# Three chained sequence models on one core: the order of the attention part rewritten, with five PSUM banks and a later copy

## The chip, the cores and the metric

The kernel runs on one core of a Trainium2 chip. Measured is the device time of one execution in microseconds; lower is better. A profile is one execution of its own, recorded by the hardware profiler; its times are the rows shown below.

## What is computed

Three models follow one another on 4 sequences of 768 positions (768 x 384 per sequence).

```python
# 1. delta-rule attention, 8 heads of 48, state 48 x 48 per head
k_n = k / (norm(k) + 1e-6)
for t in range(768):
    y[t] = q[t] @ state
    state = state + beta[t] * outer(k_n[t], v[t] - k_n[t] @ state)
# 2. Fourier mixing and an MLP
u = x + real(fft(fft(x, over positions), over features))
x = u + relu(layernorm(u) @ w_ch1) @ w_ch2          # 384 -> 1536 -> 384
# 3. token mixing with a phase, and a channel MLP
theta = x @ w_theta
u = x + w_tok_r @ (x * cos(theta)) + w_tok_i @ (x * sin(theta))
out = u + relu(u @ w_ch)
```

All in float32. Large matmuls take each operand as a high and a low part and add three products (`mm3`, L84), so weights and inputs are split first.

## The kernel before

**Attention in chunks.** The recurrence is cut into chunks of 64 positions, 12 per sequence. For each chunk the inverse of a triangular 64 x 64 matrix is needed; it is made of two 32 x 32 blocks solved at once on VectorE and joined by small matmuls. The class `Front` has one method for each kind of step, and a number says which piece it works on:

- `k`, `q`, `g` (`gram`, L228): load transposed keys (L245), multiply them with themselves (`k`), with the queries (`q`) or both (`g`), and copy the products from PSUM into the tile `KQ` on ScalarE (L252, L255, L257, L259; L261 on GpSimd). Number d = 0 to 23 is a pair of chunks for all heads; four of them make a solve. `k` of d % 4 below 2 loads into the two buffers `kt`; the others borrow the buffers `u`, which the weight pieces use as well.
- `s` (`solve`, L263): w = 0 to 5. Transposes `KQ` (L272), then runs 30 steps of two dependent VectorE instructions (L309, L312) and a last product (L313). Tiles `T`, `TN`, `TT` have one buffer, `KQ` two.
- `j` (`solved`, L317): two transposes of the result into `TN` and `TT` (L321, L323).
- `l` (`load`, L362): four loads (L368, L370) and a mask on GpSimd (L372).
- `c` (`chunks`, L375): for pair d: loads v (L384), scales it on GpSimd (L385), first product `pa` (L390), its copy to `A` (L393), copies of `TT` into `YU` (L395, by `copy`, L356, on ScalarE for d in `COPY_ACT`, else on VectorE), second product `pt` with that copy as operand (L399), more copies (L401, L402), third product `pw` (L406) and its copy (L408).
- `n` (`scan`, L410): chunk g = 0 to 47, in order: product `pu` (L425), copies (L426, L427), new state `ps` (L436) and its copies (L437, L438), outputs `py` (L447), which every second scan copies (L452, L454) and stores (L455). Scan g uses pair g // 2, and pair d the solve d // 4.
- `f`: load the Fourier constants (L470). `w1` and `W1` (`convert`, L693): split one of 24 weight pieces (`Split.steps`, L106): load 384 KB (L120), first step on ScalarE (L123), VectorE (L124 to L130), three matmuls (L132 to L134), copies (L131, L135). `W1` may be issued on an engine only behind the last instruction of the latest solve there.

**The order.** `PLAN` (L66) lists all these steps; `attention_steps` (L701) runs the list, and "|" and every twelfth scan give control back. What is listed is a rank: the framework's scheduler goes through a simulated time and, on each engine and queue, takes the instruction of the lowest rank that it believes ready. The result is a fixed order for each engine, and on the chip each engine keeps to it. The list runs until scan 11 (the first sequence); then the Fourier inputs of the first sequence are made on VectorE (`fourier_inputs`, L472), and the MLP blocks begin: 12 blocks (256 positions each) of 12 steps, each step an `ffn_up` (L666) and an `ffn_down` (L678). After each step the list is run on to its next "|" (`attend`, L754), so the rest of the attention lies between matmuls of the MLP. Pieces of weights not yet converted are converted by the loop when needed: all 24 by step 5 of block 0. `LEAD` (L58) says at which steps of a block the next block's three preparations are ranked: loads, transform and norm, and transposes (`prepare_2`, L654: L661 to L663). When the attention is done, the weights of the third model are split in the same places; then the third model follows (`TokenMix.run`).

**PSUM.** Eight banks: two for the scan, one called `mw`, three in the ring `g`, and two accumulators `pc0` and `pc1` that `ffn_down` uses from the first block on. `mw()` (L219) gives a bank to each small product of the attention: until scan 11 every third goes to `mw` and the others to the ring `g`, behind it all to `mw`. The matmuls of the weight pieces use the ring too.

Of the kernel before, what the change touches and what calls it, by code (L numbers as in the profile page):

```python
# [10 lines left out]
F32 = mybir.dt.float32  # L11
# [31 lines left out]
NKT = 2  # L43
NYT = 8
BLOCKED = 0
COPY_ACT = (0, 1, 2, 3, 4, 5)
DIAG_ACT = (0, 1)
FOFF = 0
NZ = 9
# [4 lines left out]
AHEAD = {(0, 0): 1, (0, 1): 1, (0, 2): 1}  # L54
MIXACT = False
NMW = 1
MWT = 3
LEAD = (0, 4, 11)  # L58
LEAD_0 = (5, 7, 11)
LATE = {4: 1, 7: 1, 10: 1}  # L60
MIXAT = (11, 0)
# [1 line left out]
STRIDE = 2  # L63
ACTL = 2
NST = 2
PLAN = """k0 k3 k2 k1 q2 w1 g7 q0 l0 q1 q3 f l1 g4 s0 g5 g6 j0 c0 c1 n0 n1 n2 l2 W1 W1 W1 w1  # L66
 W1 n3 c2 l3 c3 W1 W1 W1 g9 W1 W1 w1 n4 g10 W1 n5 s1 j1 l4 g8 W1 W1 g11 c4 n6 n7 W1 n8
 W1 l5 n9 l6 c5 n10 W1 W1 n11 c6 s2 | l7 c7 j2 n12 n13 n14 n15 g13 g15 l8 c8 g12 g14 l9 c9 s3
 | | n16 n17 l10 | n18 n19 l11 c10 | c11 g19 | | g17 g18 n20 n21 g16 n22 j3 l12 c12 | n23 l13 |
 c13 n24 | | n25 l14 s4 n26 c14 n27 l15 c15 | g20 g21 g22 g23 n28 n29 l16 j4 c16 s5 | n30 n31 w1 |  # L70
 l17 c17 n32 n33 | l18 c18 n34 | n35 | l19 c19 n36 j5 | | n37 | l20 n38 n39 l21 c20 c21 | n40 n41
 l22 c22 n42 | n43 l23 c23 | n44 n45 | | n46 n47"""
SCAN_UP = (0, 0)
CHUNK_UP = (0, 0)
SOLVE_UP = (0, 0)
FDVE = 2
EVERY = 1
TCARGS = {"schedule_with_timeline_sim": True}
# [80 lines left out]
class Front:  # L159
# [10 lines left out]
    B1 = [slice(r, r + 32) for r in (64, 0)]  # L170
    B2 = [slice(r + 32, r + 64) for r in (64, 0)]
    ROWS = (slice(0, 128), slice(0, 112))

    def __init__(self, tc, io, ident, x2scr):
        self.tc, self.nc, self.io, self.ident, self.x2scr = tc, tc.nc, io, ident, x2scr
        self.stage1, self.staged, self.turn, self.early, self.T = -1, 0, 0, True, {}
        self.nT, self.KQ, self.ysc, self.py, self.y, self.z, self.G = {}, {}, {}, {}, {}, {}, {}

    def open_attention(self, ctx):
# [38 lines left out]

    def mw(self, shape, name):  # L219
        self.turn += 1  # L220
        if self.early and self.turn % MWT:
            return self.psg.tile(shape, F32, tag="g", name=name)
        return self.psw.tile(shape, F32, tag="mw", name=name)

    def mm(self, o, l, r):
        self.nc.tensor.matmul(o, l, r, start=True, stop=True, skip_group_check=True)  # L226
# [129 lines left out]
    def copy(self, d, o, i):  # L356
        if d in COPY_ACT:
            self.nc.scalar.activation(o, i, AF.Copy)
# [16 lines left out]
    def chunks(self, d):  # L375

        nc, mm, sol = self.nc, self.mm, self.sol
        FE, TK, B1, B2 = self.FE, self.TK, self.B1, self.B2
        TT, TN, nT, kq = self.W
        yu, x, y3 = self.YU[d % NYU], self.X[d % NX], self.Y3[d % NY3]  # L380
        i1 = 8 * (d % 4)
        n = slice(i1, i1 + 8)
# [8 lines left out]
        A = sol.tile([P, 8, 32], F32, tag="A", name=f"A{d}", bufs=2)  # L391
        for par in range(2):
            nc.scalar.activation(A[B2[par]], pa[B2[par]], AF.Copy)  # L393
        for par in range(2):
            self.copy(d, yu[B2[par], par, :, 32:64], TT[B2[par], n, :])  # L395
        pt = self.mw([P, 8, 32], f"pt{d}")
        for i in range(8):
            for par in range(2):
                mm(pt[B1[par], i, :], A[B2[par], i, :], yu[B2[par], par, i, 32:64])  # L399
        for par in range(2):  # L400
            self.copy(d, yu[B1[par], par, :, 0:32], TT[B1[par], n, :])  # L401
            nc.scalar.activation(yu[B1[par], par, :, 32:64], pt[B1[par]], AF.Copy, scale=-1.0)  # L402
        pw = self.mw([P, 8, C], f"pw{d}")
        for i in range(8):
# [336 lines left out]
def front(tc, top, io, ident, x2scr, mix):  # L741
# [6 lines left out]
    fr.init()  # L748
    steps = fr.attention_steps(PLAN)
    state = {"fed": 0}  # L750
# [62 lines left out]
    for n, (q, f) in enumerate(order):  # L813
        more = q + 1 < len(blocks)
        lead = LEAD if q else LEAD_0
        if f in lead and more:
# [299 lines left out]
```

## Time and profile before

| | |
|---|---|
| three timed runs | 961.49, 966.62, 970.60 us; median 966.62 |
| profiled execution, time | 964.93 us |
| its span, first to last instruction | 963.2 us |
| TensorE busy, share of the span | 884.4 us, 92% |
| VectorE, ScalarE, GpSimd busy | 66%, 44%, 32% |
| mean granted TensorE clock | 0.943 of full speed |

A busy TensorE isn't one at its peak, since matmuls overlap and their ends are modelled. The clock was granted at about one half from 24 to 72 us and at full speed from about 216 us.

### The profile page before, as it was taken

The numbers are of one execution on the slowest core, as the hardware profiler recorded it, in microseconds if no ns is written. First come the engines' busy times: TensorE is split into PE (matmuls) and PEld (weight loads), VectorE is DVE, ScalarE is ACT, GpSimd is POOL, SyncE is SP. The second block draws the span as 40 slices with busy tenths as digits, with TensorE's granted clock in tenths as the row PEclk, the third lists the DMA queues.
The fourth block names the chain that finished last, engine by engine and source line by source line (L and its number), as shares of the span: only waits on it lengthen the run. The fifth ranks groups of instructions, "written<-read, shape, count | busy, mean of one in ns | idle before, by whom it ended". The sixth has DMA issues, their size and how long they took to land.

```text
span 963.2 us, 23409 instructions
## 1 busy us (share of the span) xinstructions
PE 884.4 (92%) x9408; PEld 797.8 (83%) x9408; DVE 634.0 (66%) x1490; ACT 428.5 (44%) x1072; POOL 311.8 (32%) x422
## 2 busy tenths in 40 slices
PE   4659888789999999999999998999998999999998
PEld 4547566677988898988988997888997999999987
DVE  4989879946998872698231596878657866273411
ACT  4367676445534454345535322322556345162410
POOL 1201242323123014223313155554224545143321
PEclk7557897899999999999999999999999999999999
DMA  7324352323222014011313023233121311021000
GB/s 214 105 73 137 107 167 75 109 86 121 62 87 90 19 58 147 28 55 39 92 34 109 10 83 115 69 97 116 50 84 41 89 58 37 25 59 33 25 17 33
DMA packets 42204, 73.58 MB, mean 76 GB/s; under 512 B 6000, under 2 KB 26224, under 8 KB 42096
## 3 DMA queue, kind: packets, MB, share of 16 engines
q1 hardware_dynamic: 41328, 69.72, 24.2%
q0 software_dynamic: 768, 2.36, 0.9%
q8 instruction: 74, 1.21, 0.5%
q14 instruction: 34, 0.28, 0.1%
HBM read 57.91 MB, written 14.16 MB: 75 GB/s over the span
## 4 chain that ended last, share of the span: by engine, by line
PE 52%; DVE 24%; DMA 9%; ACT 6%; issue 4%; POOL 3%; SPq 1%; ACTq 0%; DVEq 0%; POOLq 0%
PE pc L684 4%; PE ph L85 4%; PE ty L87 3%; PE ph L86 3%; PE ty L85 3%; PE pc L685 3%; PE pc L687 3%; PE ty L86 3%; PE ph L87 3%; DVE T L312 3%; DVE tmp L309 3%; PE sm L226 2%; PE py L226 2%; PE pu L226 2%; PE pw L226 2%
## 5 line engine op out<-in xcount | busy, mean ns | idle before, releaser
L85 PE MATMUL ph<-uh,w1h 128*128 128x256 f32 x432 | 124.8, 292 | 1.3 <-DVE ul L663 1.0
L86 PE MATMUL ph<-ul,w1h 128*128 128x256 f32 x432 | 123.0, 286 | 2.0 <-DVE ul L663 1.8
L87 PE MATMUL ph<-uh,w1l 128*128 128x256 f32 x432 | 121.8, 283 | 0.0
L675 DVE SCALAR_TENSOR_TENSOR hl<-ph,hh 128x256 fp32r<-128x256 f32 x144 | 59.5, 418 | 93.3 <-ACT hh L674 88.2
L684 PE MATMUL pc<-w2h,hh 128*128 128x384 f32 x288 | 103.5, 359 | 2.3 <-ACT hh L674 2.3
L685 PE MATMUL pc<-w2l,hh 128*128 128x384 f32 x288 | 97.8, 340 | 0.0
L674 ACT ACTIVATE hh<-ph 128x256 fp32r<-128x256 f32 x144 | 53.4, 380 | 89.9 <-PE ph L87 74.8
L226 PE MATMUL sm<-kt 48*64 48x128 f32 (+1 forms) x896 | 68.7, 310 | 23.0 <-DMA kt<-in_kq_dram 11.3
L86 PEld LDWEIGHTS ph<-ul,w1h 128*128 128x128 f32 x432 | 81.6, 189 | 5.1 <-DVE ul L663 3.7
L85 PEld LDWEIGHTS ph<-uh,w1h 128*128 128x128 f32 x432 | 80.9, 189 | 4.8 <-DVE ul L663 1.7
L226 PEld LDWEIGHTS sm<-kt 48*64 48x64 f32 x896 | 55.5, 171 | 34.6 <-issue 11.0
L87 PEld LDWEIGHTS ph<-uh,w1l 128*128 128x128 f32 x432 | 81.7, 189 | 0.4 <-issue 0.2
L687 PE MATMUL pc<-w2h,hl 128*128 128x384 f32 x288 | 75.5, 342 | 3.6 <-DVE hl L675 3.5
L372 POOL TENSOR_SCALAR_AFFINE_SELECT YQ<-KQ 64x512 f32<-64x512 f32 x48 | 33.8, 704 | 127.5 <-PE py L226 113.1
L309 DVE TENSOR_TENSOR tmp<-T 128x30 f32<-128x30 f32 (+9 forms) x180 | 66.9, 372 | 4.6
L312 DVE TENSOR_TENSOR T<-T,tmp 128x30 f32<-128x30 f32 (+9 forms) x180 | 65.0, 361 | 4.5
L385 POOL TENSOR_TENSOR X<-X,nT 64x384 f32<-64x384 f32 x48 | 44.6, 930 | 65.7 <-DMA X<-in_v_dram 50.5
L684 PEld LDWEIGHTS pc<-w2h,hh 128*128 128x128 f32 x288 | 54.2, 188 | 6.4 <-ACT hh L674 3.2
L685 PEld LDWEIGHTS pc<-w2l,hh 128*128 128x128 f32 x288 | 54.4, 189 | 1.3
L687 PEld LDWEIGHTS pc<-w2h,hl 128*128 128x128 f32 x288 | 49.8, 188 | 5.4 <-DVE hl L675 5.1
L261 POOL COPY KQ<-KQ 32x128 f32<-32x128 f32 x64 | 23.3, 364 | 82.8 <-ACT KQ L259 77.8
L996 POOL TENSOR_TENSOR w2l<-xT,w2h 128x384 fp32r<-128x384 f32 x24 | 25.3, 1057 | 73.2 <-ACT w2h L995 73.2
(307 smaller groups left out, 2314.0 us busy)
## 6 DMA issues: line engine op xcount, KB each, us to landing
kt<-in_kq_dram SPq DMA_DIRECT2D x48, 224.0 KB, 2.6
w_0raw<-in_w_dram SPq DMA_DIRECT2D x15, 384.0 KB, 3.3
YQ<-in_qt_dram SPq DMA_DIRECT2D x48, 96.0 KB, 3.3
Y<-in_kn_dram SPq DMA_DIRECT2D x48, 96.0 KB, 2.7
X<-in_v_dram SPq DMA_DIRECT2D x48, 96.0 KB, 2.5
ysc<-y SPq DMA_DIRECT2D x24, 192.0 KB, 2.2
x2scr<-u SPq DMA_DIRECT2D x12, 384.0 KB, 3.0
wti_0raw<-in_wti_dram SPq DMA_DIRECT2D x12, 384.0 KB, 3.2
```

Source lines behind the costliest of these rows:

```text
L85: nc.tensor.matmul(out, lh, rh, start=start, stop=False)
L86: nc.tensor.matmul(out, lh, rl, start=False, stop=False)
L87: nc.tensor.matmul(out, ll, rh, start=False, stop=stop)
L226: self.nc.tensor.matmul(o, l, r, start=True, stop=True, skip_group_check=True)
L309: nc.vector.tensor_tensor(pr, E[:, :, j + 1:, j:j + 1].to_broadcast([P, nb, n, j]), E[:, :, j, 0:j].unsqueeze(2).to_broadcast([P, nb, n, j ...
L312: nc.vector.tensor_tensor(E[:, :, j + 1:, 0:j], E[:, :, j + 1:, 0:j], pr, ALU.add)
L385: nc.gpsimd.tensor_tensor(x[TK[par], par], x[TK[par], par], nT[TK[par], n].unsqueeze(2).to_broadcast([C, 8, D]), ALU.mult)
L674: nc.scalar.activation(hh, ph, AF.Relu)
L675: self.up_end = nc.vector.scalar_tensor_tensor(hl, ph, 0.0, hh, ALU.max, ALU.subtract)
L684: nc.tensor.matmul(self.pc[i], hh[:, i * P:(i + 1) * P], wh, start=(f == 0), stop=False)
L685: nc.tensor.matmul(self.pc[i], hh[:, i * P:(i + 1) * P], wl, start=False, stop=False)
L687: nc.tensor.matmul(self.pc[i], hl[:, i * P:(i + 1) * P], wh, start=False, stop=(f == KF - 1))
```

## The change

The list is new throughout. At its start the keys come as 3, 2, 0, 1 instead of 0, 3, 2, 1; grams 7 and 6 and the queries follow; the loads of chunk 1 stand ahead of the Fourier constants and those of chunk 0 behind gram 4; the first weight piece stands behind solve 0. Grams 10, 9 and 8 stand ahead of solve 1. Of the weight pieces, 13 stand ahead of solve 1 and 19 ahead of scan 11 in both lists, and 16 (before) and 18 (after) ahead of scan 8. Behind scan 11, solves 4 and 5 stand closer together, and weight marks are added that find nothing left to convert. Besides: small products go round by `ROTA` through `mw`, the two accumulator banks and the ring, one, two and two of five; the copies of pairs 0 and 1 go to VectorE and that of pair 6 to ScalarE; the second product of a chunk reads `TT` itself, and the copy into `YU` is ranked behind it; the transposes of the next block are ranked at step 10 instead of 11.

```diff
-COPY_ACT = (0, 1, 2, 3, 4, 5)
+COPY_ACT = (2, 3, 4, 5, 6)
...
-MWT = 3
-LEAD = (0, 4, 11)
+ROTA = "mppgg"
+LEAD = (0, 4, 10)
...
-PLAN = """k0 k3 k2 k1 q2 w1 g7 q0 l0 q1 q3 f l1 g4 s0 g5 g6 j0 c0 c1 n0 n1 n2 l2 W1 W1 W1 w1
- W1 n3 c2 l3 c3 W1 W1 W1 g9 W1 W1 w1 n4 g10 W1 n5 s1 j1 l4 g8 W1 W1 g11 c4 n6 n7 W1 n8
- W1 l5 n9 l6 c5 n10 W1 W1 n11 c6 s2 | l7 c7 j2 n12 n13 n14 n15 g13 g15 l8 c8 g12 g14 l9 c9 s3
- | | n16 n17 l10 | n18 n19 l11 c10 | c11 g19 | | g17 g18 n20 n21 g16 n22 j3 l12 c12 | n23 l13 |
- c13 n24 | | n25 l14 s4 n26 c14 n27 l15 c15 | g20 g21 g22 g23 n28 n29 l16 j4 c16 s5 | n30 n31 w1 |
- l17 c17 n32 n33 | l18 c18 n34 | n35 | l19 c19 n36 j5 | | n37 | l20 n38 n39 l21 c20 c21 | n40 n41
- l22 c22 n42 | n43 l23 c23 | n44 n45 | | n46 n47"""
+PLAN = """k3 k2 k0 k1 g7 g6 q1 q0 l1 q2 q3 f g4 | l0 s0 w1 g5 j0 c0 c1 n0 W1 W1 n1 W1 l2 W1
+ w1 c2 W1 n2 n3 l3 c3 n4 W1 W1 g10 w1 W1 g9 W1 W1 g8 s1 W1 n5 j1 l4 W1 g11 c4 n6 W1 W1
+ n7 W1 n8 l5 n9 c5 n10 l6 W1 n11 l7 c6 s2 n12 c7 j2 n13 n14 l8 g13 n15 | | g15 c8 g12 g14 l9
+ c9 s3 | n16 n17 n18 n19 l11 l10 | c10 c11 g19 g17 n20 j3 n21 l12 c12 | g18 n22 | g16 n23 | l13 |
+ n24 n25 l14 c13 n26 | c14 n27 l15 | c15 w1 g23 | w1 g20 g22 n28 n29 l16 g21 s4 j4 | s5 c16 n30 n31
+ l17 c17 n32 n33 | n34 l18 | c18 | n35 l19 c19 n36 j5 | | | w1 n37 w1 w1 | l20 c20 n38 n39
+ l21 c21 n40 n41 l22 n42 | n43 l23 c22 c23 n44 n45 | | | n46 n47"""
...
+T_LATE = True
...
     def mw(self, shape, name):
         self.turn += 1
-        if self.early and self.turn % MWT:
-            return self.psg.tile(shape, F32, tag="g", name=name)
+        if self.early:
+            k = ROTA[self.turn % len(ROTA)]
+            if k == "p":
+                self.pturn = 1 - self.pturn
+                return self.psc.tile(shape, F32, tag=f"pc{self.pturn}", name=name)
+            if k == "g":
+                return self.psg.tile(shape, F32, tag="g", name=name)
         return self.psw.tile(shape, F32, tag="mw", name=name)
...
-        for par in range(2):
-            self.copy(d, yu[B2[par], par, :, 32:64], TT[B2[par], n, :])
+        if not T_LATE:
+            for par in range(2):
+                self.copy(d, yu[B2[par], par, :, 32:64], TT[B2[par], n, :])
         pt = self.mw([P, 8, 32], f"pt{d}")
         for i in range(8):
             for par in range(2):
-                mm(pt[B1[par], i, :], A[B2[par], i, :], yu[B2[par], par, i, 32:64])
+                mm(pt[B1[par], i, :], A[B2[par], i, :], TT[B2[par], i1 + i, :])
         for par in range(2):
+            if T_LATE:
+                self.copy(d, yu[B2[par], par, :, 32:64], TT[B2[par], n, :])
             self.copy(d, yu[B1[par], par, :, 0:32], TT[B1[par], n, :])
+        for par in range(2):
             nc.scalar.activation(yu[B1[par], par, :, 32:64], pt[B1[par]], AF.Copy, scale=-1.0)
```

## Rows read from the trace of the kernel before

**Rows 1.** Stages: stretch, length, then busy us and instructions by engine, clock, DMA.

```profile
20.65:60.00 39.35, 25.02 (x283) 20.67 (x284) 36.53 (x83) 14.66 (x39) 8.11 (x9) 0.50 0.34 99
60.00:106.00 46.00, 37.46 (x578) 29.37 (x576) 40.67 (x115) 35.16 (x87) 9.94 (x10) 0.65 0.40 118
106.00:168.00 62.00, 52.68 (x892) 39.56 (x890) 50.08 (x112) 41.97 (x105) 19.34 (x32) 0.89 0.38 114
...
258.00:551.00 293.00, 289.25 (x4041) 257.61 (x4041) 181.96 (x469) 131.80 (x365) 78.13 (x130) 1.00 0.22 67
551.00:717.00 166.00, 158.71 (x1064) 148.57 (x1064) 127.34 (x302) 56.39 (x142) 78.18 (x87) 1.00 0.28 83
```

**Rows 2.** Timeline up to the first solve: start, us, engine, line, [idle before <-releaser].

```profile
4.80 6.66 PE L226 MATMUL sm<-kt 48*64 48x64 f32 x128 [4.80 <-DMA kt<-in_kt_dram]
...
9.93 0.53 SPq L120 DMA_DIRECT2D w_0raw<-in_w_dram  x1
...
10.86 0.77 ACT L257 ACTIVATE KQ<-sm 32x256 f32<-32x256 f32 x2
...
17.73 0.55 ACT L123 ACTIVATE w_0ag<-w_0raw 128x384 f32<-128x384 f32 x1 [6.11 <-DMA w_0raw<-in_w_dram]
...
18.31 0.60 ACT L255 ACTIVATE KQ<-sm 128x512 f32<-128x512 f32 x1
...
19.53 1.62 PE L132 MATMUL w_0s<-w_0ag,ident 128*128 128x384 f32 x2 [6.78 <-DVE w_0ag L126]
...
20.65 1.98 DVE L272 STREAM_TRANSPOSE T<-KQ 128x1024 f32<-128x1024 f32 x1 [0.40 <-ACT KQ L257]
```

**Rows 3.** DMA issues by line: count, KB each, median us from issue to landing.

```profile
w_0raw<-in_w_dram SPq DMA_DIRECT2D x15, 384.0 KB, 3.3
```

**Rows 4.** Timeline: copies on VectorE, and solve steps alone and beside GpSimd.

```profile
189.20 2.37 DVE L360 COPY YU<-TT 32x256 f32<-32x256 f32 x8
...
83.65 0.39 DVE L312 TENSOR_TENSOR T<-T,tmp 128x228 f32<-128x228 f32 x1
...
95.29 0.91 DVE L312 TENSOR_TENSOR T<-T,tmp 128x228 f32<-128x228 f32 x1
...
93.24 3.65 POOL L385 TENSOR_TENSOR X<-X,nT 64x384 f32<-64x384 f32 x2 [3.34 <-DMA X<-in_v_dram]
```

**Rows 5.** Waits of the first 200 us: total us, times, longest us.

```profile
PE pa L226 <- ACT A L393: 5.8, 2, 4.9
```

**Rows 6.** Timeline of ScalarE around the scans, 101 to 166 us.

```profile
101.46 0.33 ACT L426 ACTIVATE X<-pu 64x192 f32<-64x192 f32 x1
...
111.80 1.70 ACT L358 ACTIVATE YU<-TT 32x256 f32<-32x256 f32 x4 [2.91 <-DVE TT L323]
...
114.30 0.30 ACT L437 ACTIVATE X<-ps 48x192 f32<-48x192 f32 x1
...
117.29 0.56 ACT L123 ACTIVATE w_768ag<-w_768raw 128x384 f32<-128x384 f32 x1 [0.90 <-DMA w_768raw<-in_w_dram]
...
122.00 0.33 ACT L426 ACTIVATE X<-pu 64x192 f32<-64x192 f32 x1
...
143.31 1.18 ACT L408 ACTIVATE YU<-pw 48x512 f32<-48x512 f32 x2
...
155.48 0.33 ACT L426 ACTIVATE X<-pu 64x192 f32<-64x192 f32 x1 [0.73 <-PE pu L226]
...
165.86 0.31 ACT L426 ACTIVATE X<-pu 64x192 f32<-64x192 f32 x1
```

**Rows 7.** Waits of TensorE from 240 to 717 us: total us, times, longest us.

```profile
PE ph L86 <- DVE ul L663: 1.8, 4, 0.9
...
PE ph L85 <- DVE ul L663: 1.0, 2, 0.6
```

**Rows 8.** Timeline of TensorE: the first product of the MLP.

```profile
199.82 0.39 PE L85 MATMUL ph<-uh,w1h 128*128 128x256 f32 x1
```

More of the change, by code (lines that the diff above doesn't have):

```diff
@@ L65 @@
 NST = 2
-PLAN = """k0 k3 k2 k1 q2 w1 g7 q0 l0 q1 q3 f l1 g4 s0 g5 g6 j0 c0 c1 n0 n1 n2 l2 W1 W1 W1 w1
- W1 n3 c2 l3 c3 W1 W1 W1 g9 W1 W1 w1 n4 g10 W1 n5 s1 j1 l4 g8 W1 W1 g11 c4 n6 n7 W1 n8
- W1 l5 n9 l6 c5 n10 W1 W1 n11 c6 s2 | l7 c7 j2 n12 n13 n14 n15 g13 g15 l8 c8 g12 g14 l9 c9 s3
- | | n16 n17 l10 | n18 n19 l11 c10 | c11 g19 | | g17 g18 n20 n21 g16 n22 j3 l12 c12 | n23 l13 |
- c13 n24 | | n25 l14 s4 n26 c14 n27 l15 c15 | g20 g21 g22 g23 n28 n29 l16 j4 c16 s5 | n30 n31 w1 |
- l17 c17 n32 n33 | l18 c18 n34 | n35 | l19 c19 n36 j5 | | n37 | l20 n38 n39 l21 c20 c21 | n40 n41
- l22 c22 n42 | n43 l23 c23 | n44 n45 | | n46 n47"""
+PLAN = """k3 k2 k0 k1 g7 g6 q1 q0 l1 q2 q3 f g4 | l0 s0 w1 g5 j0 c0 c1 n0 W1 W1 n1 W1 l2 W1
[3 more added lines that the diff above has]
+ n24 n25 l14 c13 n26 | c14 n27 l15 | c15 w1 g23 | w1 g20 g22 n28 n29 l16 g21 s4 j4 | s5 c16 n30 n31
+ l17 c17 n32 n33 | n34 l18 | c18 | n35 l19 c19 | n36 j5 | | | w1 n37 w1 w1 | l20 c20 n38 n39
+ l21 c21 n40 n41 l22 n42 | n43 l23 c22 c23 n44 n45 | | | n46 n47"""
 SCAN_UP = (0, 0)
@@ L176, in __init__ @@
         self.stage1, self.staged, self.turn, self.early, self.T = -1, 0, 0, True, {}
+        self.pturn = 0
         self.nT, self.KQ, self.ysc, self.py, self.y, self.z, self.G = {}, {}, {}, {}, {}, {}, {}
```

## The prediction, made before the changed kernel was run

> **What bounds the kernel now.** I read the table of stages first, then the timeline of the first 60 us, the waits of the first 200 us, the timeline of the scans, and last the waits of TensorE after 240 us.
>
> The stages [rows 1] fall into two kinds. In the last two, from 258 to 717 us, TensorE is busy for 289.25 of 293.00 us and for 158.71 of 166.00 us: work bounds them, and only the rest, 3.75 + 7.29 us, can be idle time to win. In the first 168 us another engine or a chain decides. From 20.65 to 60 us VectorE is busy for 36.53 of 39.35 us: that is the first solve, a serial chain. From 60 to 106 us it is busy for 40.67 of 46.00 us, with the second solve and the weight pieces between its steps. From 106 to 168 us no engine is full; there the scans follow one another. The Fourier part of the first sequence and with it the first product of the MLP (199.82 us, [rows 8]) wait for scan 11. So a microsecond taken from the chain keys, solve 0, solve 1, chunks 4 and 5, scan 11 is a microsecond of the whole, as long as the work left for TensorE behind it stays the same. It does: list and bodies do the same matmuls.
>
> The first wait on this chain stands in [rows 2]. The 128 key matmuls end at 4.80 + 6.66 = 11.46 us, and ScalarE has copied three of the four key groups by 11.63 us. Its next instruction is the first step of a weight piece, whose load was issued at 9.93 us; it starts at 17.73 us, 6.11 us idle. Only behind it come the fourth copy (18.31 us) and with that the first transpose of the solve (20.65 us). TensorE, in order too, stood 6.78 us before the same piece.
>
> The second wait lies in the scans [rows 6]: the copy that follows scan 4's first product is at 101.46 us and that of scan 5 at 122.00 us, 20.5 us, where those of scans 9 and 11 (155.48 and 165.86) are two steps of 5.2 us apart. In the hole ScalarE waits 2.91 us for a transposed solve with four copies of a chunk, and then runs copies of grams and weight pieces ahead of the state copy (114.30) and of scan 5.
>
> **The change part by part.** The sum is made against the profiled execution, 964.93 us (span 963.2 and 1.7 around it); the median of the three timed runs is 966.62, 1.7 more, and is added at the end.
>
> *Weight piece behind the first solve, keys 3 2 0 1.* If the fourth key copy goes right behind the third, it starts at 11.63 and ends after its 0.60 and 0.77 us at 13.0 us; the transpose then stands at about 13.05 instead of 20.65: -7.6 us. What is late next is the solve itself; the grams of the second solve move along, since TensorE loses its 6.78 us in the same place. The list gives only ranks: the scheduler that orders the instructions puts a lower rank first where it believes it ready sooner. That happened before too, for the piece stood behind all four keys in the old list. On SP the piece is now ranked behind the four loads of chunk 1, the three Fourier constants and the four loads of chunk 0; before, the list put it ahead of most of these, yet it was issued only at 9.93, when the stage buffer of key 3 was free. Keys 3 and 2 now come first, so both stage buffers are free a group earlier and the piece's load may be issued just as soon as before. Bounds: -7.6 us, and 0 if the weight step keeps its place. I take -7.6, for the rank now forbids what the old one only failed to prevent, and the margin was thin (fourth group ready at 11.46, ScalarE free at 11.63). The four loads of chunk 0, moved behind the grams, are wanted by the first chunk only, far behind the solve: 0.
>
> The row has 7.8 us from issue to use for a piece whose median is 3.3 [rows 3]. The Trainium skill (DMA: Bandwidth & Descriptors, Anatomy of one DMA, told there for the software path) has a transfer cost about 2.0 us and its bytes at 436 GB/s, an estimate of 2.9 us for 384 KB. By it the piece would have been there at 12.8 us, the transpose 2.9 us later as in the rows, and moving the piece would be worth 2.7 us, not 7.6; the total would be 962. The measured 7.8 us decides, in a stretch in which the two large constants were under way.
>
> *Copies of chunks 0 and 1 from ScalarE to VectorE, those of chunk 6 the other way.* Eight copies on VectorE took 2.37 us [rows 4]. They come due between the two solves, where VectorE is the full engine: +2.4 us if they push the second solve, 0 if its end isn't what the scans wait for (chunk 4 used its transposes 20 us late, see the hole). I take +1.2. Chunk 6 lies behind scan 11: 0.
>
> VectorE's step on 128x228 took 0.39 us alone and 0.91 beside a GpSimd multiply that ran from 93.24 for 3.65 us [rows 4]. The Trainium skill (SBUF, State Buffer, Who interferes with whom) says that GpSimd and VectorE take turns at a shared port pair, a copy between SBUF tiles among the holders. The trace agrees for the solve's steps; no row shows it for the copies. If each of the eight lost the same 0.52 us, 4.2 us would come on top, and the total would be 961 instead of 957.
>
> *Second product reads the solved triangle itself, copy behind it.* Two copies of 0.425 us (1.70 for four, [rows 6]) leave the path of each chunk; on the chain are chunks 4 and 5: -1.7 to 0, the copies now wait behind the product and may delay what is next. I take -0.9.
>
> *Five banks in turn.* Before, one early product in three took the single small bank and two took the ring of three; now two in five go to the two accumulator banks, idle until the first block. The waits that an emptied bank ends are those of the chunk's first product on the copy of an earlier one, 5.8 us in two [rows 5]. Both lie beside the second solve, so most is covered: -5.8 to +2 (more in flight puts more copies into ScalarE's queue). I take -2.
>
> *List between the solves and scan 11.* 19 weight pieces stand ahead of scan 11 in both lists and 13 ahead of solve 1, but 18 instead of 16 ahead of scan 8. A piece has three steps on ScalarE, and the first took 0.56 us [rows 6]; with 1.7 us for the three, two pieces ahead of the scan's copies are +3.4 us at most; they are gone from behind it, so 0 at least. I take +1. The order of grams 8 to 10 ahead of solve 1 frees nothing that the rows show.
>
> *Transposes of the next block one step sooner (10 for 11).* They end the waits for the low half of the input: 1.8 + 1.0 us after 240 us [rows 7]. -2.8 to +1, as they now take ring banks from the products of the step; I take -1.5.
>
> *List behind scan 11.* The weight marks there have nothing left to convert. Solves 4 and 5 move beside each other and scans are spread otherwise, on a TensorE that is full: -3.75 (all its idle time) to +7.3 (as much again as stands idle behind the attention); I take 0.
>
> Sum: -7.6 + 1.2 - 0.9 - 2 + 1 - 1.5 = -9.8 us. 964.93 - 9.8 = 955.1; with the 1.7 to the median 956.8 us.
>
> **The rivals.**
>
> *The piece stays ahead of the fourth key (the list doesn't do what it says).* For it: it was behind it in the old list too, and the load can be issued as soon. Against: keys 2 and 3 first leave the fourth copy no other predecessor. Price: the 7.6 us are missing, 964.4 us.
>
> *The hole between scans 4 and 5 closes.* For it: five banks, and no copies ahead of the second product to hold ScalarE at 111.80. Against: TensorE and ScalarE must do the same grams and pieces somewhere. 20.5 - 5.2 = 15.3 us are in it, but scan 8 needs chunk 4, whose last copy is at 143.31; I count 10 of them: 947 us.
>
> *A new hole opens, and the change is slower.* One mechanism: ScalarE takes its instructions in order, and with two more pieces ahead of scan 8 and more products in flight a state copy comes to stand behind a copy whose input is late. Place: scans 4 to 8. Price: one more hole as the one seen, 15.3 us, 972 us. It decides from the point where scan 11's first copy stands later than at 165.86 us although solve 0 began sooner. Against it: the banks ease this very place.
>
> **How the numbers follow.** Forecast 0.40, piece stays 0.30, hole closes 0.17, new hole 0.13. The forecast's own range is 950 to 962. A measurement of this kernel can tell about 1% from no change, 957.0 on the one side and 976.3 on the other. Faster: 0.26 of the forecast, 0.17 of the closing hole and 0.02 of the rest, 0.45. Slower by over 1% needs the hole and one of the upper bounds (copies beside GpSimd, a fuller second half): 0.12 with what the forecast's bounds add. No change: 0.43. The range for 8 in 10 goes from below the closed hole, 943, to the single new hole, 972.
>
> **What would show it.** The first transpose of the solve at about 13 us, with no wait of ScalarE for a weight load ahead of it; solve 0 as long as before (some 34 us), solve 1 beginning at about 53 to 55 us; the chunk's wait of 5 us at a bank gone; scan 11's first copy at about 158 us instead of 165.86, and the first product of the MLP at about 192 us instead of 199.82; from there every stage as long as before. Wrong would be: the transpose still near 20 us; the front shorter but the stage from the first product to the last block longer by the same, since work was only deferred; or gains in the second half, where I count none.

## The result, and the profile after

The changed kernel takes 958.95 us (median of 16 runs, 955.61 to 966.12) beside 968.69 us for the kernel before (16 runs in the same series): a ratio of 0.9911 with a 95% interval of 0.9894 to 0.9928, some 0.9% faster. (The ratios of this document are taken from all executions of a series and aren't quotients of two medians; here those would give 0.9899.) The profiled execution took 958.93 us, its span is 957.2 us (963.2 before). The forecast was 956.8 us in a range of 943 to 972, so the number holds. Its working does not: the largest term never came about, and what the runs can trace of the gain lies in a place where I counted nothing.

The table of stages of the changed kernel, in the columns of [rows 1]:

```profile
20.65:60.00 39.35, 25.11 (x298) 21.00 (x300) 36.53 (x83) 14.68 (x40) 8.06 (x9) 0.54 0.33 103
60.00:106.00 46.00, 37.44 (x546) 27.41 (x542) 38.31 (x112) 29.92 (x73) 4.65 (x5) 0.72 0.38 113
106.00:168.00 62.00, 55.18 (x862) 42.02 (x858) 46.35 (x114) 42.92 (x108) 21.38 (x35) 0.72 0.37 117
...
258.00:551.00 293.00, 290.32 (x4073) 260.39 (x4072) 191.95 (x484) 135.88 (x377) 81.30 (x136) 1.00 0.22 68
551.00:717.00 166.00, 162.28 (x1083) 152.26 (x1081) 130.23 (x298) 57.78 (x141) 77.59 (x83) 1.00 0.31 92
```

Compare the last two with [rows 1]. TensorE stands idle for 2.68 us instead of 3.75 in the first and for 3.72 instead of 7.29 in the second: 4.6 us of the 6.0 that the span lost. The first solve's stage reads as before, VectorE 36.53 us busy in both.

The start, as in [rows 2] (every line of the changed file is 1 to 11 higher: L123 is L124, L226 is L233, L255 and L257 are L262 and L264, L272 is L279):

```profile
10.06 0.53 SPq L121 DMA_DIRECT2D w_0raw<-in_w_dram  x1
10.31 0.60 ACT L262 ACTIVATE KQ<-sm 128x512 f32<-128x512 f32 x1 [0.31 <-PE sm L233]
...
16.64 0.55 ACT L124 ACTIVATE w_0ag<-w_0raw 128x384 f32<-128x384 f32 x1 [5.73 <-DMA w_0raw<-in_w_dram]
...
17.21 0.76 ACT L264 ACTIVATE KQ<-sm 32x256 f32<-32x256 f32 x2
...
18.76 0.60 ACT L262 ACTIVATE KQ<-sm 128x512 f32<-128x512 f32 x1
...
20.19 1.96 DVE L279 STREAM_TRANSPOSE T<-KQ 128x1024 f32<-128x1024 f32 x1 [1.02 <-ACT KQ L264]
```

The list ranks the weight piece behind the solve, yet ScalarE still takes its first step ahead of the last key copies, and now even between the two copies of the third group (10.31 and 17.21). It waits 5.73 us there where it waited 6.11, and the first transpose of the solve stands at 20.19 us instead of 20.65. The step still stands in its way.

VectorE between the first two solves, and the first transpose of the second one's result:

```profile
60.07 2.41 DVE L367 COPY YU<-TT 32x256 f32<-32x256 f32 x8
...
62.67 1.90 DVE L279 STREAM_TRANSPOSE T<-KQ 128x1024 f32<-128x1024 f32 x1
...
119.54 1.99 DVE L328 STREAM_TRANSPOSE TN<-T 128x1024 f32<-128x1024 f32 x1
```

The first copies of the scans on ScalarE, scans 4, 5, 6 and 11, to be read beside [rows 6] (there scan 6 is the row 128.65 below, from the kernel before):

```profile
128.65 0.33 ACT L426 ACTIVATE X<-pu 64x192 f32<-64x192 f32 x1
```

```profile
113.86 0.33 ACT L437 ACTIVATE X<-pu 64x192 f32<-64x192 f32 x1
...
120.12 0.33 ACT L437 ACTIVATE X<-pu 64x192 f32<-64x192 f32 x1
...
135.88 0.33 ACT L437 ACTIVATE X<-pu 64x192 f32<-64x192 f32 x1
...
167.77 0.33 ACT L437 ACTIVATE X<-pu 64x192 f32<-64x192 f32 x1 [1.94 <-PE pu L233]
```

The hole of 20.5 us between scans 4 and 5 is 6.3 us now, but the next interval, which was 6.7 us (122.00 to 128.7), is 15.8. The hole went one scan on. Scan 11 stands 1.9 us later than before in this profile, but that isn't shown to come from the change. Two kernels of the experiments below, old_tail and lead11_back, run the same instructions in the same order as the changed kernel on VectorE, ScalarE and GpSimd up to the first MLP product. They have the hole in the same two intervals, yet scan 11 at 168.83 and 161.35 us. Three others share the front of the kernel before in this sense and have it at 161.35 to 165.72.

Chunk 4's first product before the change, then the two first products of chunks that wait for a solve's transposes in the changed kernel, for [rows 5], and the waits of TensorE from 240 to 717 us, for [rows 7]:

```profile
132.36 0.69 PE L226 MATMUL pa<-TN,KQ 32*32 32x32 f32 x32
```

```profile
57.56 1.06 PE L233 MATMUL pa<-TN,KQ 32*32 32x32 f32 x32 [5.28 <-DVE TN L328]
...
121.59 0.69 PE L233 MATMUL pa<-TN,KQ 32*32 32x32 f32 x32 [2.47 <-DVE TN L328]
```

```profile
PE pt L672 <- DVE hl L686: 1.9, 2, 1.3
PE pt L672 <- DVE un L662: 1.4, 2, 0.9
...
PE ph L86 <- DVE ul L674: 0.3, 1, 0.3
...
PE ph L87 <- DVE ul L674: 0.2, 1, 0.2
```

The wait for a bank (5.8 us of `pa` for `A`) is gone from the list. `pa` now waits 5.28 us for the transposes of the first solve (3.69 before), and 2.47 us, where it had none, for those of the second, which come at 119.54 instead of 107.8. The waits for the low half fell from 2.8 to 0.5 us, while the transposes themselves now wait 1.9 us for `hl` and 1.4 us for `un` (0.9 for `hl` before, and none listed for `un`): 2.4 us more, so what the products no longer wait, the transposes do.

TensorE from the end of the scans to the first product of the MLP, the second row for [rows 8]:

```profile
180.91 1.97 PE L233 MATMUL sm<-kt 48*64 48x128 f32 x16 [5.64 <-ACT YU L419]
...
202.54 0.39 PE L86 MATMUL ph<-uh,w1h 128*128 128x256 f32 x1
```

So in this pair of profiles the front is 2.7 us longer, and the gain lies behind it. But the 2.7 us are not shown to be the change's work: the kernels with the same front as before have their first product at 196.87 to 200.45 us, those with the changed front at 198.49 to 202.54. Up to the first product TensorE even stood idle for less, 47.78 instead of 51.52 us, and was busy for longer, 154.76 instead of 148.30 us, with 2266 matmul instructions instead of 2261 and at a mean granted clock of 0.71 instead of 0.74.

For every kernel of this study I read four moments from the timeline: scan 11's first copy; the first MLP product; the first product of the ninth block (the products stand in 12 groups of 108, L85 to L87); the end of the span. One profiled execution each, in us. Each ratio is against the kernel before in the same series of runs; its median was 964.8 to 965.8 us in the later series and 968.69 in the first, the only one in which the changed kernel ran:

| kernel | scan 11 | first product | from there to block 9 | from there to the end | ratio to before, 95% |
|---|---|---|---|---|---|
| before | 165.86 | 199.82 | 384.4 | 379.0 | 1 |
| lead10_only | 165.72 | 199.07 | 387.5 | 377.0 | 0.9978 (0.9959 to 0.9998) |
| old_list | 163.46 | 201.37 | 386.9 | 375.9 | 1.0038 (1.0014 to 1.0061) |
| new_list_only | 165.89 | 203.47 | 383.9 | 378.4 | 1.0015 (0.9994 to 1.0035) |
| new_tail | 163.24 | 200.45 | 379.7 | 378.4 | 0.9957 (0.9934 to 0.9980) |
| bar_dropped | 161.35 | 196.87 | 381.6 | 377.6 | 0.9935 (0.9911 to 0.9959) |
| late_and_bar | 166.06 | 211.87 | 382.6 | 379.6 | 1.0084 (1.0053 to 1.0116) |
| old_tail | 168.83 | 202.41 | 381.6 | 378.2 | 0.9999 (0.9976 to 1.0021) |
| late_off | 162.36 | 203.38 | 378.8 | 377.7 | 1.0019 (0.9993 to 1.0046) |
| lead11_back | 161.35 | 198.49 | 377.4 | 379.5 | 0.9932 (0.9907 to 0.9956) |
| piece_held | 169.74 | 209.81 | 376.5 | 378.9 | 1.0027 (1.0005 to 1.0050) |
| piece_held_2 | 159.08 | 204.92 | 375.6 | 381.4 | 0.9980 (0.9960 to 1.0000) |
| piece_and_solve_held | 160.90 | 202.91 | 386.0 | 379.5 | 0.9995 (0.9971 to 1.0018) |
| after | 167.77 | 202.54 | 375.8 | 378.9 | 0.9911 (0.9894 to 0.9928) |

After against before: +2.7 in the front, -8.6 in the first eight blocks, -0.1 behind, together -6.0 us of span. In those eight blocks TensorE's idle time fell from 9.0 to 4.8 us; 3.0 of these 4.2 us are in the seventh and eighth. The other 4.4 us are busy time, which there is shorter and in the front longer, by 6.5.

### The profile page after: what moved, and what is told of

It reads as the page before. It is cut to its first block, busy times and chain, and to the rows that moved or that the text cites. A ratio compares the mean times of both kernels' runs of the same rounds, so it can differ in the third digit from the quotient of the medians.

```text
span 957.2 us, 23429 instructions
## 1 busy us (share of the span) xinstructions
PE 887.4 (93%) x9408; PEld 800.8 (84%) x9408; DVE 635.1 (66%) x1494; ACT 426.9 (45%) x1068; POOL 307.8 (32%) x422
## 4 chain that ended last, share of the span: by engine, by line
PE 60%; DVE 21%; DMA 6%; ACT 6%; issue 4%; POOL 2%; SPq 0%; ACTq 0%; DVEq 0%; POOLq 0%
PE ph L86 4%; PE pc L695 4%; PE ph L88 4%; PE ph L87 4%; PE pc L698 4%; PE pc L696 4%; PE ty L87 3%; PE ty L88 3%; PE ty L86 3%; PE sm L233 3%; DVE tmp L316 3%; DVE T L319 3%; DMA w_0raw<-in_w_dram 3%; PE pg L554 2%; PE pm L630 2%
## 5 line engine op out<-in xcount | busy, mean ns | idle before, releaser
L87 PE MATMUL ph<-ul,w1h 128*128 128x256 f32 x432 | 122.5, 284 | 0.3 <-DVE ul L674 0.2
L695 PE MATMUL pc<-w2h,hh 128*128 128x384 f32 x288 | 101.0, 351 | 0.6 <-ACT hh L685 0.6
L233 PE MATMUL sm<-kt 48*64 48x128 f32 (+1 forms) x896 | 68.8, 310 | 26.4 <-DMA kt<-in_kq_dram 14.9
L233 PEld LDWEIGHTS sm<-kt 48*64 48x64 f32 x896 | 55.6, 171 | 39.3 <-DMA kt<-in_kq_dram 8.6
L87 PEld LDWEIGHTS ph<-ul,w1h 128*128 128x128 f32 x432 | 81.5, 189 | 2.0 <-DVE ul L674 0.9
L698 PE MATMUL pc<-w2h,hl 128*128 128x384 f32 x288 | 77.6, 345 | 0.1
L392 POOL TENSOR_TENSOR X<-X,nT 64x384 f32<-64x384 f32 x48 | 41.9, 874 | 57.2 <-DMA X<-in_v_dram 52.3
```

What stands on the lines that cost most here:

```text
L87: nc.tensor.matmul(out, lh, rl, start=False, stop=False)
L392: nc.gpsimd.tensor_tensor(x[TK[par], par], x[TK[par], par], nT[TK[par], n].unsqueeze(2).to_broadcast([C, 8, D]), ALU.mult)
L695: nc.tensor.matmul(self.pc[i], hh[:, i * P:(i + 1) * P], wh, start=(f == 0), stop=False)
L698: nc.tensor.matmul(self.pc[i], hl[:, i * P:(i + 1) * P], wh, start=False, stop=(f == KF - 1))
```

## The experiments

**One step sooner, alone and undone.** Kernel lead10_only is the kernel before with this one line; lead11_back is the changed kernel without it.

```diff
-LEAD = (0, 4, 11)
+LEAD = (0, 4, 10)
```

> The kernel before with one edit, the next block's transposes ranked at step 10 instead of 11. Theory S (the sooner transposes carry the gain, since in the profile of after the blocks behind the attention are 7 us shorter while the first product of the MLP comes 2.7 us later): 5 to 8 us faster than before, about 962, the gain all behind 500 us. Theory L (the list carries it, as the attention ends at 535 instead of 542 us): within 2 us of before. My own figure in the prediction was 1.5 us.

Measured: 964.08 us, ratio 0.9978, so some 2.1 us (0.22% of 965.7).

> The changed kernel with the transposes back at step 11, all else new. Theory S: 5 to 8 us slower than after, about 965. Theory L: within 2 us of after, about 959.

Measured: 958.28 us, ratio 0.9932 where the whole change has 0.9911; the intervals overlap, and the median is not above the changed kernel's 958.95. Alone the line is worth about 2 us (0.2 to 4), near the 1.5 that I took; in the changed kernel no worth is shown. It doesn't carry the change: theory L, not S.

**The list out of the change, and the list alone.** Kernel old_list is the changed kernel with the old `PLAN`, everything else kept; new_list_only is the kernel before with the new `PLAN` and nothing else.

> The changed kernel with the old list in it; banks, late copy, copies' engines and step 10 stay new. Theory S: within 3 us of after, about 959 to 962, with the blocks behind 551 us as short as in after. Theory L: 6 to 9 us slower than after, about 966, with the attention ending at about 542 us again.

> The kernel before with the whole new list and nothing else: old banks, copies and step. If the list alone makes the gain, 959 or less, 1% below before. If it needs the five banks or the late copy, within 3 us of before.

Measured: 969.42 us (1.0038) and 966.05 us (1.0015). Without the list the other edits lose, more than theory L said; without the other edits the list gains nothing. Neither half holds any of the 0.9%: they work together only.

**The first key group really first.** Kernel piece_held fixes what the list does not: the weight piece's steps are held, on ScalarE, behind the copy of the last key, on VectorE behind the solve.

```diff
+                first = not self.done
+                with ExitStack() as hold:
+                    if first:
+                        hold.enter_context(self.tc.issue_after(self.key_copy.ins))
+                        hold.enter_context(self.tc.issue_after(self.solve_end.ins))
```

> The changed kernel with the first weight piece really held: its ScalarE steps behind the last key copy, its VectorE steps behind the end of solve 0. If the start is on the path of the whole, as my prediction had it, the first transpose stands at about 13 us instead of 20.2, and the whole is 5 to 7 us faster than after, about 953. If the scans and TensorE's queue decide in the front, solve 0 ends 7 us sooner and the first product of the MLP stays within 3 us of 202.5; the whole then within 3 us of after.

Measured: 969.04 us, 1.0027: over 1% slower than the changed kernel, which neither case of the expectation allowed for. ScalarE's last key copy, the steps of pieces behind it and the square root of the solve, and VectorE's first instructions of the solve, in this kernel:

```profile
12.44 0.76 ACT L264 ACTIVATE KQ<-sm 32x256 f32<-32x256 f32 x2
16.56 0.55 ACT L124 ACTIVATE w_0ag<-w_0raw 128x384 f32<-128x384 f32 x1 [3.35 <-DMA w_0raw<-in_w_dram]
19.83 0.55 ACT L124 ACTIVATE w_0ag<-w_0raw 128x384 f32<-128x384 f32 x1 [2.73 <-DMA w_0raw<-in_w_dram]
...
21.60 0.23 ACT L300 ACTIVATE s<-dg 128x32 f32<-128x32 f32 x1
```

```profile
13.24 1.90 DVE L281 STREAM_TRANSPOSE T<-KQ 128x1024 f32<-128x1024 f32 x1 [4.59 <-ACT KQ L264]
...
21.86 0.18 DVE L301 TENSOR_SCALAR s<-s 128x32 f32<-128x32 f32 x1 [6.50 <-ACT s L300]
```

The transpose stands at 13.24 us, where the forecast had it (13.05). Then VectorE waits 6.50 us for the square root on ScalarE, which stands behind two steps of pieces that wait 3.35 and 2.73 us for their loads, and behind the copies of a gram. The stall was moved by a few instructions.

Kernel piece_held_2 holds all that too: solve 0 ranked right behind the keys, and ScalarE's part of grams and pieces behind the square root (`sqrt0` is that instruction).

```diff
-PLAN = """k3 k2 k0 k1 g7 g6 q1 q0 l1 q2 q3 f g4 | l0 s0 w1 g5 j0 c0 c1 n0 W1 W1 n1 W1 l2 W1
+PLAN = """k3 k2 k0 k1 s0 g7 g6 q1 q0 l1 q2 q3 f g4 | l0 w1 g5 j0 c0 c1 n0 W1 W1 n1 W1 l2 W1
...
+            hold.enter_context(self.tc.issue_after(self.sqrt0.ins))
```

> The changed kernel with solve 0 ranked behind the keys and everything else that ScalarE does, grams and weight pieces, behind that solve's square root (in the first attempt the square root itself came to stand behind a piece and a gram whose loads were late). The solve then begins at about 13 us and ends at about 47 instead of 53. If the chain of the front decides, as my prediction had it, the first product of the MLP comes 5 to 7 us sooner than in after and the whole is at about 953. If the loads of the grams and the Fourier inputs decide, solve 1 begins sooner by less than 3 us and the whole is within 3 us of after.

Measured: 963.46 us, 0.9980: hardly better than before the change (the interval reaches 1), and 0.7% behind the changed kernel. Neither case of the expectation covers that: solve 1 begins 4.5 us sooner (58.18 instead of 62.67), and the time is longer. Solve 0's last product now starts at 45.50 us instead of 53.19 in the changed kernel, and scan 11's first copy is at 159.08, where the profiles with the changed front have 161.35 to 168.83. The first MLP product is no sooner all the same (204.92, for 198.49 to 202.54). This is where it went, rows of the three engines:

```profile
171.79 1.23 DVE L322 TENSOR_TENSOR T<-T,g 128x1024 f32<-128x1024 f32 x1
...
175.83 1.11 DVE L494 TENSOR_TENSOR y<-y,y 128x385 f32<-128x385 f32 x2
```

```profile
177.03 0.53 ACT L510 ACTIVATE y<-y 128x385 f32<-128x385 f32 x1 [12.96 <-issue]
```

```profile
178.38 2.01 PE L233 MATMUL pw<-YU,Y 64*48 64x64 f32 x32 [13.49 <-ACT YU L415]
```

I call it the hand-over. The adds that make the Fourier inputs stand on VectorE between and behind the last steps of solve 2, which end at 171.79 + 1.23 us. ScalarE's first Fourier step (L510) stands idle for 12.96 us; its row names no releaser, but it scales what such an add writes, and it starts 0.09 us after the pair of adds of 175.83 ends. Behind it on ScalarE stands a chunk's copy, and TensorE's next matmul needs that one: 13.49 us idle. Three engines in order, each waiting at its head. With the front of the kernel before, the wait was 4.99 us (3.22 to 8.25 in the four profiles), with the changed front 5.64 (5.36 to 10.63 in three).

**The hand-over taken away.** Kernel piece_and_solve_held is the last one with solve 2's VectorE steps from the 18th on held behind the last Fourier add.

```diff
+            with self.tc.issue_after(self.fourier_end.ins) if w == 2 and j == HOLD2 else nullcontext():
```

> The changed kernel with the first solve's keys really first (as in the run before: solve 0 ranked behind the keys, the weight pieces' and grams' work on ScalarE behind its square root, on VectorE behind its end) and, besides, the steps of solve 2 from step 18 on behind the last Fourier input of the first sequence on VectorE. Theory Q (the front gives the time back since VectorE does solve 2 ahead of the Fourier inputs): with that out of the way the first product of the MLP comes at 190 to 195 us instead of 202.5 and the time is 948 to 954, ratio 0.980 to 0.986. Rival (another queue takes its place: solve 2 is then late for the chunks of the second sequence, or ScalarE stands at another input): first product 195 to 203 us, or the blocks of the first sequence idle by what the front gained; 957 to 963, ratio 0.990 to 0.996.

Measured: 966.62 us, 0.9995; theory Q fails, and what the rival describes is seen, though the time lies above its range too. The profile is of one of the longest of its 12 executions (970.10 us). The wait at the hand-over fell to 2.21 us, but the solve, ending 16 us later, now lies on VectorE among the norms of the first block:

```profile
188.06 1.23 DVE L324 TENSOR_TENSOR T<-T,g 128x1024 f32<-128x1024 f32 x1
189.20 0.16 DVE L662 RECIPROCAL rs<-sd 128x2 f32<-128x2 f32 x1
189.32 2.14 DVE L332 STREAM_TRANSPOSE TN<-T 128x1024 f32<-128x1024 f32 x1
191.35 1.91 DVE L334 STREAM_TRANSPOSE TT<-T 128x1024 f32<-128x1024 f32 x1
193.11 0.15 DVE L663 TENSOR_TENSOR rs<-rs,ve 128x2 f32<-128x2 f32 x1
```

```profile
199.16 0.90 PE L678 MATMUL pt<-ident,un 128*128 128x128 f32 x3 [7.25 <-DVE un L668]
```

Two steps of the norm (189.20 and 193.11) have the solve's two transposes between them, and TensorE waits 7.25 us for the norm's result. The first product stays at 202.91, and the blocks up to the ninth take 386.0 us, for 375.6 in piece_held_2; that the later solve does this is likely, and wasn't tested.

**The end of the list.** In new_tail the kernel before gets only the new list's end, from behind `j5`; in old_tail the changed kernel gets the old end.

```diff
-  n36 j5 | | n37 | l20 n38 n39 l21 c20 c21 | n40 n41 l22 c22 n42 | n43 l23 c23 | n44 n45 | | n46 n47
+  n36 j5 | | | w1 n37 w1 w1 | l20 c20 n38 n39 l21 c21 n40 n41 l22 n42 | n43 l23 c22 c23 n44 n45 | | | n46 n47
```

> The kernel before with only the end of its list replaced by that of the new one (all behind j5: there scans 40 to 42 and chunk 21 stand in the same section as scans 38 and 39, so they are ranked before the rule that holds scan 40 back for the third sequence's Fourier transform is asked). In the four profiles so far the three blocks of the third sequence have 17 us of TensorE time beyond the matmuls' usual pitch with the old list and 9 with the new, and all of the gain. Theory G (the end of the list does it): 6 to 9 us faster than before, about 958. Theory M (the middle of the list does it, solves 3 to 5 and their grams): within 2 us of before.

> The changed kernel with the end of the old list behind j5. Theory G: 6 to 9 us slower than after, about 966, the first block of the third sequence 7 us longer. Theory M: within 2 us of after, about 958.

Measured: 961.15 us (0.9957) and 965.29 us (0.9999). The end of the list alone is 0.4% faster, and taking it out of the change costs 0.9%: theory G holds, though alone the end brings some 4 us where G said 6 to 9. (The whole new list in the old kernel gave 1.0015, so its first part costs some 0.6% there, 1.0015 / 0.9957, which the other edits have to win back. In the diff of the change, the line of the new list that begins with `l17` lacks a mark: the kernel has a "|" between `c19` and `n36`.) The clean test of its mechanism is one mark. `attend` (L754) asks once for each section whether a scan of the second half of a sequence may be listed (L761): scans 40 to 47 only when the third sequence's first stage has come. A section that begins below scan 40 is let through whole.

```diff
- l17 c17 n32 n33 | l18 c18 n34 | n35 | l19 c19 n36 j5 | | n37 | l20 n38 n39 l21 c20 c21 | n40 n41
+ l17 c17 n32 n33 | l18 c18 n34 | n35 | l19 c19 n36 j5 | | n37 | l20 n38 n39 l21 c20 c21 n40 n41
```

> The kernel before, with one mark taken out of its list: the "|" between chunk 21 and scan 40. Nothing else differs; the steps and their order are the same. Theory G (the gate): the second half of the scans is held back, section by section, until the first stage of the third sequence has come, so a scan that shares its section with scans 38 and 39 is let through with them, and one behind a "|" waits. Then scans 40 to 42 are ranked sooner, the attention ends sooner (542.8 us before; 535 to 540 expected), TensorE's stretch from 551 to 717 us stands idle less, and the time falls by 4 to 8 us: ratio 0.992 to 0.996. Rival (it is the sections' other contents, the solves 4 and 5 beside each other, chunk 23 or the empty marks): no more than 2 us, ratio 0.998 to 1.002.

Measured: 960.00 us, 0.9935, some 6.3 us for one character. ScalarE's first copies of scans 39 and 40 and its last outputs, before:

```profile
464.17 0.33 ACT L426 ACTIVATE X<-pu 64x192 f32<-64x192 f32 x1 [1.34 <-PE pu L226]
...
486.44 0.33 ACT L426 ACTIVATE X<-pu 64x192 f32<-64x192 f32 x1
...
542.43 0.33 ACT L452 ACTIVATE y<-py 128x192 f32<-128x192 f32 x1 [1.00 <-PE py L226]
```

and without the mark:

```profile
462.99 0.33 ACT L426 ACTIVATE X<-pu 64x192 f32<-64x192 f32 x1 [1.34 <-PE pu L226]
...
470.56 0.33 ACT L426 ACTIVATE X<-pu 64x192 f32<-64x192 f32 x1
...
529.91 0.33 ACT L452 ACTIVATE y<-py 128x192 f32<-128x192 f32 x1 [2.17 <-PE py L226]
```

Scan 40 follows scan 39 after 7.6 us instead of 22.3, and the attention ends 12.5 us sooner. In the profiles 2.8 of the gain lie between first product and ninth block; the first product is 2.9 us earlier in this one execution too, though no step ahead of it was changed, so the median and not the profile says what the mark is worth. TensorE's idle time from 258 to 717 us is 8.9 us instead of 11.0 [rows 1], and 6.4 in the changed kernel.

**The late copy out of the change.** Kernel late_off is the changed kernel with the switch off, and `pt` reading `YU` again. The loop that the change split in two, so that both copies of `TT` stand ahead of both copies of `pt`, stays split.

```diff
-T_LATE = True
+T_LATE = False
...
-                mm(pt[B1[par], i, :], A[B2[par], i, :], TT[B2[par], i1 + i, :])
+                mm(pt[B1[par], i, :], A[B2[par], i, :], yu[B2[par], par, i, 32:64])
```

> The changed kernel with the second product of a chunk reading the copy in YU again, and the copy ranked ahead of it, as before the change. Theory C (the copies carry what the list alone did not bring): the list alone left the time at 966 us, the whole change at 959; if the late copy is most of these 7 us, the time is 963 to 967, ratio 0.996 to 1.000, and the first product of the MLP stands later than 202.5 us or the blocks of the first sequence idle more. Rival 1 (my own term, two copies of 0.425 us off the path of two chunks): +0.9 us, ratio 0.991 to 0.994. Rival 2 (banks carry it, since more products in flight is what the rearranged list needs): no difference, ratio 0.990 to 0.992.

Measured: 967.51 us, 1.0019. Some 1.1% (1.0019 / 0.9911) hangs on this edit, by itself as much as the whole change gains. Its profile doesn't show why. Scan 11 stands at 162.36 us there and the wait at the hand-over is 10.61 us, where the changed kernel's profile has 167.77 and 5.64:

```profile
180.97 1.97 PE L233 MATMUL sm<-kt 48*64 48x128 f32 x16 [10.61 <-ACT YU L419]
```

But lead11_back, which has the late copy and the changed kernel's front, has scan 11 at 161.35 us and the same wait:

```profile
177.88 1.97 PE L233 MATMUL sm<-kt 48*64 48x128 f32 x16 [10.63 <-ACT YU L419]
```

So the longer wait is no sign of the missing late copy. The profile is also of the fastest of the 12 executions (961.60 us), and the other 6 us to the median can't be read from it.

**The late copy with the mark, in the old list.** Kernel late_and_bar is the kernel before with these two edits only; here the late copy comes together with the split of that loop.

> The kernel before with two small edits and nothing else of the change: the "|" between chunk 21 and scan 40 taken out, and the second product of a chunk reading TT itself with its copy into YU ranked behind it. The mark alone gave 0.9935; the late copy, taken out of the whole change, cost some 1.1% (0.9911 to 1.0019). Theory A (the late copy is worth that by itself): the two add up to about 16 us, 948 to 952 us, ratio 0.981 to 0.986, and this is the fastest kernel of the study. Theory B (the late copy is needed only beside the rearranged list, which made the chunks later; the old list has no place where it decides): as the mark alone or 1 to 2 us better, 957 to 961 us, ratio 0.990 to 0.995. A ratio above 0.997 would mean that the late copy hurts the old order.

Measured: 974.02 us, 1.0084, the slowest of all. Where the late copy saves 1.1% in the new list, here it costs, with the split of the loop, 1.5% (1.0084 / 0.9935); neither theory had that sign, though the last sentence names it. VectorE, ScalarE and TensorE at the hand-over, without the late copy (bar_dropped):

```profile
172.65 0.55 DVE L498 SCALAR_TENSOR_TENSOR y<-y,t 128x385 f32<-128x385 f32 x1
...
182.32 1.23 DVE L313 TENSOR_TENSOR T<-T,g 128x1024 f32<-128x1024 f32 x1
```

```profile
175.43 1.97 PE L226 MATMUL sm<-kt 48*64 48x128 f32 x16 [7.92 <-ACT YU L408]
```

and with it:

```profile
179.62 1.23 DVE L313 TENSOR_TENSOR T<-T,g 128x1024 f32<-128x1024 f32 x1
...
187.51 0.54 DVE L498 SCALAR_TENSOR_TENSOR y<-y,t 128x385 f32<-128x385 f32 x1
```

```profile
186.46 0.53 ACT L497 ACTIVATE y<-y 128x385 f32<-128x385 f32 x1 [14.67 <-issue]
```

```profile
190.14 1.97 PE L226 MATMUL sm<-kt 48*64 48x128 f32 x16 [17.04 <-ACT YU L408]
```

The order on VectorE is turned round: without it the Fourier step of L498 stands some 10 us ahead of the solve's last product, with it 8 us behind. TensorE waits 17.04 us instead of 7.92, and the first MLP product is at 211.87 instead of 196.87: 15.0 of the 17.9 us between the two spans. That is well outside the 196.87 to 200.45 of the four profiles with the old front.

## Why the number held and the steps did not

- *Weight piece behind the first solve, -7.6.* This step failed. The forecast said that the rank "now forbids what the old one only failed to prevent"; a rank forbids nothing, and the scheduler took the piece ahead of the key copies again. That is the first rival (0.30), whose mechanism the profile shows; its price alone would have given 964.4 us. "The transpose still near 20 us" was also named as a sign of being wrong. The step failed a second time where I had taken it for certain: that a microsecond taken from this chain is one of the whole. When the transpose was brought to 13.24 us, or solve 0's last product forward by 7.7, the square root, the hand-over and the norms took it back.
- *Copies of pairs 0 and 1, +1.2.* The eight copies (2.41 us) stand right ahead of the second solve's first transpose, 62.67 instead of 60.3, so for the start of that solve the upper bound of +2.4 is the better reading. GpSimd was idle beside them, so the doubt about the shared port was not put to the test. The transposes of that solve's result come 11.7 us later than before, much more than the copies cost. The trace shows what stretched it: from its first transpose to its last product VectorE ran 53 steps of weight pieces (23.6 us) instead of 39 (17.3 us) and stood idle for 9.2 us instead of 4.1. My term for the list up to scan 11 (+1) counted ScalarE's steps and took the pieces around solve 1 as unchanged. But most of it falls into slack, as my lower bound had it: chunk 4's first product ran at 132.36 us, over 20 us behind the transposes, and now runs at 121.59, right behind them. At this chunk the longer solve costs no more than the 2.47 us of wait.
- *Second product from the triangle itself, -0.9.* Mis-sized by more than ten times, since I priced the copy's own 0.425 us: the edit is worth -1.1% in one list and +1.5% in the other. It changes the order on the engines far from the copy, as the rows of late_and_bar show for the old list; how it gains in the new one is open.
- *Five banks, -2.* The wait that I named is gone (5.8 us); the same product's waits for the transposes are 5.28 and 2.47 us, for 3.69 before. The banks were not undone alone, nor was the exchange of copies; what each of these two is worth beside the list is open.
- *Transposes one step sooner, -1.5.* Right in size where it stands alone, about 2 us; not shown in the changed kernel. Its reason fails: the waits only changed their place.
- *List behind scan 11, 0.* The term that was mis-sized the other way. I bounded its gain by the 3.75 us of idle TensorE ahead of 551 us and set the 7.29 us behind it down as a loss only. In the change its end is worth 0.9%, and in the old list one mark that lets scans 40 to 42 through gives 0.65% alone. I had the gate's line before me and read the marks as spreading only. The change announces "solves closer together"; in the old list it was the mark. In the new list the mark was not tried alone, only the whole end.
- *Rivals.* The hole between scans 4 and 5 shrank from 20.5 to 6.3 us but went to the next interval. The condition of the slower rival, scan 11 later than 165.86, is met in this one profile by 1.9 us; another with the same front has 161.35, so it tells nothing, and the kernel is not slower.

The forecast named "gains in the second half, where I count none" as what would prove it wrong; that is what old_tail and bar_dropped show. 7.6 us expected from the start of the kernel, which never came, and some 0.9% that hangs on the far end of its list make the same total by chance.

Of the 0.9%, the runs show the end of the list and the late copy each to be needed: without either, nothing is left. They do not add up to the whole, nor does the list alone, and no row was found that carries the late copy's share in the new list. No kernel of the study has a lower ratio than the changed one, but two are not told apart from it: lead11_back (0.9932), and bar_dropped (0.9935), the kernel before without one mark. So beyond that mark the whole rewriting is not shown to have gained anything.

## What to carry to other kernels

A list of ranks is not an order: before a moved step is priced, look in the new trace whether it has moved, and what stands behind it in the same queue. Where several engines work in order and feed each other, a microsecond won upstream can't be counted until the next hand-over has been followed, engine by engine, to the wait that ends last. The edits here, which act through a scheduler, don't add, and one changed its sign with the list that it met, so test each by taking it out of the finished version as well as by putting it alone into the old one. And compare profiles of kernels with the same order in a stretch before a difference of one profile in it is explained: here they lay up to 7.5 us apart at scan 11.

## What had not been expected of the hardware

The first weight piece (384 KB) took 6.58 us from its issue at 10.06 us to the first step that uses it, after 7.8 us before the change, while the median of such loads is 3.3 us [rows 3]. The Trainium skill (DMA: Bandwidth & Descriptors, Anatomy of one DMA) has a cost, told there for one load on the software path, that gives an estimate of 2.9 us; the trace disagrees in both profiles at this place. In the changed kernel the keys had landed by 7.73 us and the second large constant by 12.28, and loads of chunks were under way besides. From the piece's issue to its use the core's DMA engines moved 259 GB/s (253 before), where the mean over the kernel is 77 (76).

The granted clock of the stage from 106 to 168 us was 0.72 of full speed in the changed kernel's profile and 0.89 before [rows 1], a mixture of 1.2 and 2.4 GHz; in the stage ahead of it TensorE had been busy for 37.44 and 37.46 of 46.00 us, so that stage doesn't tell the two apart. At the lower clock TensorE was busy for 55.18 us with 862 matmul instructions, at the higher for 52.68 us with 892, which aren't the same ones. And 16 executions of the same changed kernel spread over 10.5 us, with a mean clock of 0.951 in one of 956.38 us and 0.929 in that of 966.12: the differences of a single profile, as in the table above, are to be read with several microseconds of doubt, and the medians carry the verdicts.
